# GateLoop attention and a squared-ReLU block on one core: a complex product summed on VectorE instead of TensorE, and a planner that charges TensorE for its stops

## The chip, the cores and the metric

The kernel runs on one core of a Trainium2 chip. The core has TensorE (PE in the profile), VectorE (DVE), ScalarE (ACT), GpSimd (POOL) and SyncE (SP), each with a queue of its own that is worked off in order, and 16 DMA engines that all queues share. The metric is the device time of one execution in microseconds, lower is better; the time before is 726.08 us, the median of three runs (725.42, 726.08 and 728.75).

## What is computed

A complex recurrence runs over 768 time steps, for 4 batches of 8 heads of 48 channels. Its result, reshaped to 3072 tokens of 384 values, goes through two matrix products with a squared ReLU between them. The weights come as float64 and everything else as float32.

```python
scale = np.minimum(mag, 0.999) / (mag + 1e-06)        # mag = |a|
a_re_n, a_im_n = (a_re * scale, a_im * scale)
for t in range(S):
    ar, ai = (a_re_n[:, :, t, :, None], a_im_n[:, :, t, :, None])
    new_re = ar * S_re - ai * S_im
    new_im = ar * S_im + ai * S_re
    kv = np.einsum('bhd,bhe->bhde', k[:, :, t], v[:, :, t])
    S_re, S_im = (new_re + kv, new_im)
    y[:, :, t] = np.einsum('bhd,bhde->bhe', q[:, :, t], S_re)
...
h = x @ w_in                     # x: (3072, 384), w_in: (384, 2048)
r = np.maximum(h, 0.0)
g = r * r
return (g @ w_out).astype(np.float32)
```

## The kernel before

The 3072 tokens are cut into six units of 512 tokens (`NU = 6`). A unit has 128 blocks of four time steps; a block is a partition, and its four steps times 384 channels lie along the free axis, in two halves of heads (z = 0 and 1). Each unit goes through three stages.

**The chain** (`chain`, line 882) makes the running product of the complex decays. `roots`, `normalise` and `inner` work within the blocks, on VectorE and ScalarE, and leave each block's total in the tile `xn`, real part in row 0 and imaginary part in row 1. What is then wanted is the running product of these totals over the 128 blocks, a product along partitions. So `totals` turns `xn` on TensorE (three transposes for each of the two rows, line 1008, with a permutation in place of the identity, so that the blocks come out sorted for a scan); ScalarE copies the turned totals to `e`; `scan` multiplies them up on VectorE in levels, in many small instructions (lines 1121 to 1177); and its last level multiplies `e` (four groups of partial products) by `incx` (the prefix of each group). This last product is complex: each of its two rows is a sum of two real products. `last` (line 1184) forms them with four multiplications of 128x384 and writes the two terms of each row apart, into `gg`, which lies in `KC[0]`. It puts them down in the order of the blocks, and for that the elements that one instruction writes one after the other lie 16 elements apart. `back` then turns each row back to one block per partition, and adds the two terms at the same time: `turned` (line 1000) issues, for each of three pieces of 128 columns, two ordinary matmuls with the identity that accumulate in PSUM (line 1011). ScalarE copies the result to `xn` (line 1205). `apply` (lines 1243, 1247, 1250, 1257) multiplies it into decays, queries and keys, and `gather` (line 1297) regroups the keys by DMA into `KC`.

**The pairs** (`pairs`, four pairs of heads) compute the linear attention: transposes of q and k (`turn_pe`, line 1356, with a ScalarE copy at 1360, for units 0 and 1; DMAs for the others), scores (1374) masked on VectorE (1377), states (`keep`, 1402, 1411, 1413), and the outputs (`mix`, 1426 and 1430), which ScalarE copies to `yt` (1436) and DMAs carry to `xT` (1444).

**The dense part** (`dense`) takes the unit in two groups of 256 tokens: 16 x 3 matmuls of 128x256 with the first weights (1466), squared ReLU on ScalarE (1497, 1498), and the second product, in 32 matmuls of 128x384 per group for unit 0 (1512), and in matmuls of 128x192 with sums on VectorE (`half` at 1563, `put` at 1578, `add` at 1587) for the others. In unit 0 the weights are converted from float64 as they arrive (`convert`: ScalarE at 788 and 792, VectorE at 794, 798, 801).

No scheduler orders any of this. Every piece of work is a **step** with a cost in microseconds, written by hand (`plan.add`), the keys that it reads and writes, and a rank. `Plan.order` runs through the steps as a list scheduler does: an engine takes, of the steps whose inputs are done, the one with the lowest rank (PAIR 1, CHAIN 2, DENSE 3; the dense part's relu, copies and sums 0), and the order in which it takes them becomes the order of the engines' queues. So a cost in the plan doesn't change how long anything takes; it changes which instruction stands before which. A step of TensorE with an input from another engine counts as ready only `MARGIN` 0.6 us after that input (`SLACK` 2 us after some DMAs), beside a `HOP` for each engine. The dense matmuls of unit n have the lowest rank on TensorE, and so fill the places where the chain and the pairs of unit n+1 leave TensorE free.

```python
step("PE", 0.12 * NM * len(terms), keys, [(b,)], go, rk)                    # turned
step("DVE", 2 * tt(384) + 0.55, E + I, [("KC", 0, "r", r)] + ([] if r else K), last, ahead)
```

Of the kernel before, what the change touches and what calls it, by code (L numbers as in the profile page):

```python
# [15 lines left out]
ALU = mybir.AluOpType  # L16
# [464 lines left out]
class Plan:  # L481
# [3 lines left out]
    MARGIN = 0.6  # L485
    SLACK = 2.0
    RATE = 280e3

    def __init__(self):
        self.steps = []  # L490
# [25 lines left out]
    def order(self):  # L516
        steps = self.steps
        users = [[] for _ in steps]
        left = []
        for n, s in enumerate(steps):  # L520
            left.append(len(s[2]))
            for d in s[2]:
                users[d].append(n)
        engines = {s[0] for s in steps}
        free = {e: 0.0 for e in engines}
        wait = {e: [] for e in engines}
        done, start, at = {}, {}, {}
        bus = 0.0

        def ready(n):  # L530
            e = steps[n][0]
            t = 0.0
            for d in steps[n][2]:
                same = steps[d][0] == e and steps[d][5] is None
                hop = 0.0 if same else self.HOP[steps[d][0]]
                if e == "PE" and not same and done[d] > 100.0:
                    paired = steps[d][5] is not None and steps[n][6]
                    hop += self.SLACK if paired else self.MARGIN
                t = max(t, done[d] + hop)
            at[n] = t  # L540
            wait[e].append(n)

        for n in range(len(steps)):
            if not left[n]:
                ready(n)
        for _ in steps:
            best = None
            for e in engines:
                if not wait[e]:
                    continue  # L550
                t = max(free[e], min(at[n] for n in wait[e]))
                if best is None or t < best[0]:
                    best = (t, e)
            t, e = best
            n = min((n for n in wait[e] if at[n] <= t), key=lambda n: (steps[n][4], n))
            wait[e].remove(n)
            _, dur, _, _, _, wire, _ = steps[n]
            start[n] = t
            free[e] = t + dur
            if wire is None:  # L560
                done[n] = t + dur
            else:
                lat, size = wire
                bus = max(bus, t + dur) + size / self.RATE
                done[n] = max(bus, t + dur) + lat
            for m in users[n]:
                left[m] -= 1
                if not left[m]:
                    ready(m)
        self.start, self.done = start, done  # L570
        return sorted(start, key=lambda n: (start[n], n))
# [10 lines left out]
def fast_path(ctx, tc, q, k, v, a_re, a_im, moe_w_in, moe_w_out, out, flag):  # L582
# [6 lines left out]
    C = 128  # L589
# [5 lines left out]
    DM = H * D  # L595
    FF = moe_w_in.shape[1]
    NM = DM // C
# [13 lines left out]
    dve, pool, act, sp = nc.vector, nc.gpsimd, nc.scalar, nc.sync  # L611
    pe = nc.tensor
# [5 lines left out]
    def sb(name, n, dtype=F32, rows=C):  # L618
# [9 lines left out]
    DH = DM // 2  # L628
# [3 lines left out]
    KC = [sb(f"KC{z}", W * HH * R) for z in range(2)]  # L632
    vv = [sb("v0", W * H * D), TT[:, 2 * NT * DH:]]
    e = sb("e", 3 * DM).rearrange("p (r w g) -> p r w g", r=3, w=4)
    el = sb("el", 3 * NM).rearrange("p (r m) -> p r m", r=3)
    x = sb("x", NM * (C + 1)).rearrange("p (m c) -> p m c", m=NM)
# [4 lines left out]
    xn = sb("xn", 3 * DM).rearrange("p (r n) -> p r n", r=3)  # L641
# [12 lines left out]
    ident = sb("ident", C)  # L654
    perm = sb("perm", C)
# [12 lines left out]
    bank = {n: psum.tile([C, 512], F32, name=n)  # L668
            for n in ("d0", "d1", "d2", "sc0", "sc1", "tr0", "tr1", "yp")}
# [30 lines left out]
    def tt(n):  # L700
        return n / 960.0 + 0.07
# [9 lines left out]
    def step(*args, **kw):  # L711
        return plan.add(*args, **kw)
# [159 lines left out]
    def chain(n):  # L872
# [9 lines left out]
        ahead = (CHAIN, n - 0.01)  # L882
# [114 lines left out]
        fresh = ps_[0][3] == 0  # L997
        ends = ps_[-1][3] + ps_[-1][1] * W == S

        def turned(terms, put, by, keys, rk):  # L1000
            b = trs[slot["tr"] % 2]
            slot["tr"] += 1

            def go():
                for m in range(NM):
                    dst = put(bank[b][:, 0:DM], m)
                    if len(terms) == 1:
                        pe.transpose(dst, terms[0](m), by)
                    else:
                        for i, src in enumerate(terms):  # L1010
                            pe.matmul(dst, lhsT=src(m), rhs=by, start=(i == 0),  # L1011
                                      stop=(i == len(terms) - 1))
            step("PE", 0.12 * NM * len(terms), keys, [(b,)], go, rk)
            return bank[b][:, 0:DM], (b,)

        def natural(t, m):
# [3 lines left out]
            return t.rearrange("p (y m k) -> p m y k", m=NM, k=8)[:, m]  # L1020

        def totals(j):
            ps, b = turned([lambda m: xn[:, j, ts(m, C)]], spread, perm,
                           [("xn", j, 0), ("xn", j, 1)], ahead)
            p4 = ps.rearrange("p (w g) -> p w g", w=4)
            last = ps.rearrange("p (y m k) -> p y m k", m=NM, k=8)[:, 0, :, 0]
            step("ACT", ac(DM), [b], [("e", j)], lambda: act.copy(
                out=e[:, j], in_=p4), ahead)
            if j == 1:
                step("ACT", ac(DM), [b], [("e", 2)], lambda: act.mul(  # L1030
                    out=e[:, 2], in_=p4, mul=-1.0), ahead)
            if not ends:
                step("ACT", ac(NM), [b], [("el", j)], lambda: act.copy(
                    out=el[:, j], in_=last), ahead)
                if j == 1:
                    step("ACT", ac(NM), [b], [("el", 2)], lambda: act.mul(
                        out=el[:, 2], in_=last, mul=-1.0), ahead)

            def start():
                first = SCALE if j == 0 else 0.0  # L1040
                head = e[:, j, 0].rearrange("p (x m k) -> p x m k", x=4, m=NM)[:, 0]
                if fresh:
                    dve.memset(head[:, :, 0], first)
                else:
                    dve.tensor_copy(out=head[:, :, 0], in_=ce[:, j])
                if cross:
                    dve.memset(head[:, :, 4], first)
            step("DVE", 0.12, [("ce",)], [("e", j)], start, ahead)
# [90 lines left out]
        def scan():  # L1139
# [37 lines left out]
                dve.tensor_copy(out=x4[:, 0:2, 0], in_=tx[:, 0:2])  # L1177
                minus(incx)
            step("DVE", 0.36, I, I, finish_inc, ahead)

            for r in range(2):
                def last(r=r):
                    for f, y, ro in ((gg[0], 0, r), (gg[1], 2 - r, 1 - r)):
                        dve.tensor_tensor(
                            out=f[:, r].rearrange("p (g x w) -> p w x g", x=4, w=4),
                            in0=e[:, ro].rearrange("p w (x g) -> p w x g", x=4),
                            in1=incx[:, y].rearrange("p (x g) -> p x g", x=4).unsqueeze(
                                1).to_broadcast([C, 4, 4, 24]), op=ALU.mult)
                step("DVE", 2 * tt(384) + 0.55, E + I, [("KC", 0, "r", r)] + ([] if r else K),
                     last, ahead)  # L1190
            if not ends:
                tail = [f.rearrange("p r (m k y) -> p r m k y", m=NM, k=8)[:, :, :, 7, 15]
                        for f in gg]
                tl = few[:, 0:6].rearrange("p (r m) -> p r m", r=2)
                step("DVE", 0.15, K + [("KC", 0, "r", 0), ("KC", 0, "r", 1)], [("tl",)],
                     lambda: dve.tensor_tensor(out=tl, in0=tail[0], in1=tail[1], op=ALU.add),
                     ahead)
                product(ce, tl, lambda lo, hi: el[:, lo:hi],
                        [("tl",), ("el", 0), ("el", 1), ("el", 2)], [("ce",)],
                        few[:, 6:18], [("tl",)], late[1])  # L1200

        def back(j):
            terms = [lambda m, f=f: f[:, j, ts(m, C)] for f in gg]
            ps, b = turned(terms, natural, ident, K + [("KC", 0, "r", j)], ahead)
            step("ACT", ac(DM), [b], [("xn", j, 0), ("xn", j, 1)], lambda: act.copy(  # L1205
                out=xn[:, j], in_=ps), ahead)

# [368 lines left out]
    def put(n, o, x0, x1, op, h):  # L1576
        sl = slice(4 * h, 4 * h + 4)
        step("DVE", tt(4 * C), gk(x0, h) + gk(x1, h), gk(o, h), lambda: dve.tensor_tensor(  # L1578
            out=g4[:, o, sl], in0=g4[:, x0, sl], in1=g4[:, x1, sl], op=op), (0, n))
# [4 lines left out]

    def add(n, o, c, c0, b, o0=None):
        o0 = o if o0 is None else o0
        step("DVE", tt(DH) + 0.1, [("ot", o0, c0), (b,)], [("ot", o, c)], lambda: dve.tensor_tensor(  # L1587
            out=ots[o][:, ts(c, DH)], in0=ots[o0][:, ts(c0, DH)], in1=bank[b][:, 0:DH],
            op=ALU.add), (0, n))

# [158 lines left out]
```

## Time and profile before

| | |
|---|---|
| median of three runs | 726.08 us |
| the profiled execution: its own time | 726.25 us |
| the profiled execution: span, first to last instruction | 724.4 us |
| PE busy, of the span | 654.7 us (90%), 4226 records |
| DVE busy | 573.3 us (79%), 1176 records |
| ACT busy | 360.2 us (50%), 579 records |
| POOL busy | 176.3 us (24%), 333 records |
| PE L1011, the matmuls that turn and add | 144 records |
| DVE L1184, the multiplications of the last product | 24 records, 17.2 us, mean 814 ns |
| granted TensorE clock, mean | 0.982 |

The records of an engine are its instructions as the profiler saw them; one float32 matmul leaves two records, a transpose one. A group's line gives the count, the busy time, the mean duration of one record and the idle time of the engine just ahead of it. Successive records of one engine overlap: a PE record of 128x128 lasts 272 ns, while the next one begins after about 0.11 us. The distance from start to start is then what an instruction takes from its engine, and a merged row of the timeline with so many records gives it when the next row's start is subtracted. The chain of waits lists such distances directly. Line numbers here and below are those of the kernel before.

### The profile page before, as it was taken

The numbers are of one execution on the slowest core, as the hardware profiler recorded it, in microseconds if no ns is written. First come the engines' busy times: TensorE is split into PE (matmuls) and PEld (weight loads), VectorE is DVE, ScalarE is ACT, GpSimd is POOL, SyncE is SP. The second block draws the span as 40 slices with busy tenths as digits, with TensorE's granted clock in tenths as the row PEclk, the third lists the DMA queues.
The fourth block names the chain that finished last, engine by engine and source line by source line (L and its number), as shares of the span: only waits on it lengthen the run. The fifth ranks groups of instructions, "written<-read, shape, count | busy, mean of one in ns | idle before, by whom it ended". The sixth has DMA issues, their size and how long they took to land.

```text
span 724.4 us, 11842 instructions
## 1 busy us (share of the span) xinstructions
PE 654.7 (90%) x4226; PEld 589.5 (81%) x4226; DVE 573.3 (79%) x1176; ACT 360.2 (50%) x579; POOL 176.3 (24%) x333
## 2 busy tenths in 40 slices
PE   0037789899999999999999999999999999999996
PEld 0036678668778998999999998998999989999995
DVE  5987999899879589788899588998797997356621
ACT  6783457965575704448613658423578142122230
POOL 6504154052400003314036050033050033041100
PEclk9995899999999999999999999999999999999999
DMA  9731359320531004744018661027460045287400
GB/s 287 243 122 46 75 132 251 110 66 18 156 106 28 1 12 107 185 115 132 1 36 216 148 130 41 1 66 190 129 164 1 1 118 130 59 319 252 171 1 27
DMA packets 56358, 79.55 MB, mean 110 GB/s; under 512 B 10945, under 2 KB 38465, under 8 KB 56289
## 3 DMA queue, kind: packets, MB, share of 16 engines
q0 software_dynamic: 15232, 40.72, 18.6%
q1 hardware_dynamic: 36928, 32.98, 18.0%
q10 hardware_dynamic: 4128, 4.98, 2.7%
q8 instruction: 36, 0.59, 0.4%
q14 instruction: 34, 0.27, 0.1%
HBM read 48.76 MB, written 4.72 MB: 74 GB/s over the span
## 4 chain that ended last, share of the span: by engine, by line
PE 83%; DVE 6%; ACT 4%; SPq 1%; DMA 1%; issue 1%; DVEq 0%; ACTq 0%
PE d L1466 30%; PE d L1563 26%; PE sc L1374 5%; PE d L1512 5%; PE tr L1402 3%; PE yp L1426 3%; PE tr L1011 2%; PE yp L1430 2%; SPq L1297 1%; PE sc L1466 1%; DMA xT<-yt 1%; PE tr L1356 1%; PE d L1356 1%; DVE f L947 1%; PE tr L1466 1%
## 5 line engine op out<-in xcount | busy, mean ns | idle before, releaser
L1466 PE MATMUL d<-xT,w 128*128 128x256 f32 x1056 | 238.1, 382 | 4.5 <-DMA xT<-yt 3.4
L1466 PEld LDWEIGHTS d<-xT,w 128*128 128x128 f32 x1056 | 199.2, 191 | 32.2 <-issue 4.5
L1563 PE MATMUL d<-w,g 128*128 128x192 f32 x768 | 132.4, 327 | 0.0
L1563 PEld LDWEIGHTS d<-w,g 128*128 128x128 f32 x768 | 125.1, 190 | 0.9 <-issue 0.6
L1497 ACT ACTIVATE g<-d 128x512 f32<-128x512 f32 x88 | 52.5, 597 | 127.0 <-PE d L1466 113.8
L1297 POOL DMA_DIRECT2D KC<-f x160 | 78.7, 499 | 120.4 <-DVE f L1257 46.5
L1578 DVE TENSOR_TENSOR g<-g 128x512 f32<-128x512 f32 x64 | 43.4, 688 | 35.2 <-ACT g L1498 23.5
L868 POOL DMA_DIRECT2D v<-in_v_dram x80 | 47.0, 594 | 86.7 <-PE yp L1430 47.2
L1563 PE MATMUL d<-T,g 128*128 128x192 f32 x384 | 67.1, 326 | 0.0
L1524 POOL DMA_DIRECT2D out_dram<-ot x22 | 12.6, 573 | 207.5 <-DVE ot L1587 111.8
L1563 PEld LDWEIGHTS d<-T,g 128*128 128x128 f32 x384 | 62.9, 190 | 0.2 <-issue 0.2
L1498 ACT ACTIVATE g<-g 128x512 f32<-128x512 f32 x96 | 60.7, 633 | 3.1
L1374 PE MATMUL sc<-QT 96*128 96x128 f32 x368 | 47.9, 285 | 1.3 <-ACT QT L1360 1.3
L1374 PEld LDWEIGHTS sc<-QT 96*128 96x128 f32 x368 | 45.1, 198 | 4.4 <-ACT QT L1360 2.2
L1243 DVE TENSOR_TENSOR f<-aq,xn 128x384 f32<-128x384 f32 (+1 forms) x64 | 45.2, 751 | 1.9 <-ACT xn L1205 1.9
L1436 ACT COPY yt<-yp 112x512 f32<-112x512 f32 x24 | 26.3, 1095 | 40.0 <-PE yp L1430 40.0
L1257 DVE TENSOR_TENSOR f<-aq 128x384 f32<-128x384 f32 (+1 forms) x64 | 45.4, 753 | 0.7
L1512 PE MATMUL d<-w,g 128*128 128x384 f32 x128 | 43.9, 489 | 1.6 <-DVE w L801 1.6
L1587 DVE TENSOR_TENSOR ot<-ot,d 128x192 f32<-128x192 f32 x64 | 21.8, 350 | 25.9 <-PE d L1563 25.0
L1377 DVE TENSOR_TENSOR A<-sc,mask 128x512 f32<-128x512 f32 x45 | 30.0, 682 | 10.8 <-PE sc L1374 10.6
L947 DVE TENSOR_TENSOR f<-aq 128x384 f32<-128x384 f32 x72 | 37.0, 555 | 1.0
L1512 PEld LDWEIGHTS d<-w,g 128*128 128x128 f32 x128 | 23.3, 190 | 15.3 <-DVE w L801 2.0
(193 smaller groups left out, 1012.5 us busy)
## 6 DMA issues: line engine op xcount, KB each, us to landing
QT<-aq SPq DMA_DIRECT2D x128, 64.0 KB, 2.1
f<-in_moe_w_in_dram POOLq DMA_DIRECT2D x8, 768.0 KB, 7.4
f<-in_moe_w_out_dram POOLq DMA_DIRECT2D x8, 768.0 KB, 5.1
KC<-f POOLq DMA_DIRECT2D x104, 48.0 KB, 2.3
out_dram<-ot POOLq DMA_DIRECT2D x22, 192.0 KB, 2.6
QT<-aq ACTq DMA_DIRECT2D x64, 64.0 KB, 2.3
v<-in_v_dram POOLq DMA_DIRECT2D x80, 48.0 KB, 3.5
xT<-yt SPq DMA_DIRECT2D x36, 96.0 KB, 2.4
```

What stands on the lines that cost most here:

```text
L868: lambda i=i, c=c, src=src: pool.dma_start(out=t[32 * c:32 * c + 32, i], in_=src[c]), vrank, 32 * 1536, 4.0,
L947: dve.tensor_tensor(out=f, in0=a[:, :, :, c - 1], in1=a[:, j, :, c].unsqueeze(1).to_broadcast([C, 2, HH, D]), op=ALU.mult)
L1243: lambda j=j, r=r: dve.tensor_tensor(out=f4[:, j, r], in0=a[:, r], in1=over(j), op=ALU.mult), late[z])
L1257: lambda j=j, r=r, o=o: dve.tensor_tensor(out=o[:, :, :, r * D:(r + 1) * D], in0=qk[:, j], in1=a[:, r], op=ALU.mult), late[z])
L1297: lambda i=i, c=c, queue=queue: queue.dma_start(out=kc[32 * c:32 * c + 32, i], in_=nat[32 * i:32 * i + 32, c]),
L1374: pe.matmul(sa[:, j], lhsT=T[:, j, 1, h], rhs=T[:, j, 0, h], start=True, stop=True)
L1466: pe.matmul(ps, lhsT=w1[:, f // FP, m, ts(f % FP, C)], rhs=xT[:, n % 2, m, ts(grp, G)], start=(m == 0), stop=(m == NM - 1))
L1497: act.activation(out=o, in_=ps, func=AF.Relu)
L1498: act.activation(out=o, in_=o, func=AF.Square)
L1512: pe.matmul(ps, lhsT=gt[:, f % 2, ts(i, C)], rhs=w2[:, f], start=(f == 0), stop=(f == NF - 1))
L1563: pe.matmul(bank[b][:, 0:DH], lhsT=g4[:, r, j], rhs=w(j), start=first and j == 0, stop=last and j == NT - 1)
L1578: step("DVE", tt(4 * C), gk(x0, h) + gk(x1, h), gk(o, h), lambda: dve.tensor_tensor(out=g4[:, o, sl], in0=g4[:, x0, sl], in1=g4[:, x1, sl] ...
```

## The change

It has three parts.

1. **The last product.** `last` now writes its two terms in the scan's own order, one element after the other, and a third VectorE instruction adds them, writing the sum to `xn` in the order of the blocks. The step's cost in the plan goes from `2 * tt(384) + 0.55` to `3 * tt(384) + 0.28`, and both rows now name the whole of `K` among the keys that they write. `back` turns `xn` instead of two terms: `turned` has one source, so it issues three transposes for a row instead of six accumulating matmuls, and its cost in the plan goes from 0.72 to 0.36. The carry for the next unit (`tl`) becomes a copy from `xn` instead of an addition (line 1196).
2. **The planner.** When a TensorE step would start more than 2.5 us after the end of the one before, it and those that follow within 3.4 us are charged up to double their cost, in the plan alone.
3. **A cost.** The sums of the dense part (`add`, line 1587) are planned at 0.01 us above `tt(192)` instead of 0.1.

```diff
@@ class Plan
+    STOP, COLD = 2.5, 3.4
@@ Plan.order
-        bus = 0.0
+        bus = warm = 0.0
...
             start[n] = t
+            if e == "PE":
+
+                if t > free[e] + self.STOP:
+                    warm = t + self.COLD
+                if t < warm:
+                    dur += min(dur, 0.5 * (warm - t))
             free[e] = t + dur
@@ chain
-        def turned(terms, put, by, keys, rk):
+        def turned(src, put, by, keys, rk):
...
                 for m in range(NM):
-                    dst = put(bank[b][:, 0:DM], m)
-                    if len(terms) == 1:
-                        pe.transpose(dst, terms[0](m), by)
-                    else:
-                        for i, src in enumerate(terms):
-                            pe.matmul(dst, lhsT=src(m), rhs=by, start=(i == 0),
-                                      stop=(i == len(terms) - 1))
-            step("PE", 0.12 * NM * len(terms), keys, [(b,)], go, rk)
+                    pe.transpose(put(bank[b][:, 0:DM], m), src(m), by)
+            step("PE", 0.12 * NM, keys, [(b,)], go, rk)
@@ scan
             for r in range(2):
                 def last(r=r):
-                    for f, y, ro in ((gg[0], 0, r), (gg[1], 2 - r, 1 - r)):
+                    own = [f[:, r].rearrange("p (w x g) -> p w x g", w=4, x=4) for f in gg]
+                    for o, y, ro in ((own[0], 0, r), (own[1], 2 - r, 1 - r)):
                         dve.tensor_tensor(
-                            out=f[:, r].rearrange("p (g x w) -> p w x g", x=4, w=4),
-                            in0=e[:, ro].rearrange("p w (x g) -> p w x g", x=4),
+                            out=o, in0=e[:, ro].rearrange("p w (x g) -> p w x g", x=4),
                             in1=incx[:, y].rearrange("p (x g) -> p x g", x=4).unsqueeze(
                                 1).to_broadcast([C, 4, 4, 24]), op=ALU.mult)
-                step("DVE", 2 * tt(384) + 0.55, E + I, [("KC", 0, "r", r)] + ([] if r else K),
-                     last, ahead)
+
+                    dve.tensor_tensor(
+                        out=xn[:, r].rearrange("p (g x w) -> p w x g", x=4, w=4),
+                        in0=own[0], in1=own[1], op=ALU.add)
+                step("DVE", 3 * tt(384) + 0.28, E + I, K + [("xn", r, 0), ("xn", r, 1)], last,
+                     ahead)
             if not ends:
-                tail = [f.rearrange("p r (m k y) -> p r m k y", m=NM, k=8)[:, :, :, 7, 15]
-                        for f in gg]
+                tail = xn[:, 0:2].rearrange("p r (m k y) -> p r m k y", m=NM, k=8)[:, :, :, 7, 15]
...
-                     lambda: dve.tensor_tensor(out=tl, in0=tail[0], in1=tail[1], op=ALU.add),
+                     lambda: dve.tensor_copy(out=tl, in_=tail), ahead)
@@ back
-            terms = [lambda m, f=f: f[:, j, ts(m, C)] for f in gg]
-            ps, b = turned(terms, natural, ident, K + [("KC", 0, "r", j)], ahead)
+            ps, b = turned(lambda m: xn[:, j, ts(m, C)], natural, ident,
+                           [("xn", j, 0), ("xn", j, 1)], ahead)
@@ add
-        step("DVE", tt(DH) + 0.1, [("ot", o0, c0), (b,)], [("ot", o, c)], lambda: dve.tensor_tensor(
+        step("DVE", tt(DH) + 0.01, [("ot", o0, c0), (b,)], [("ot", o, c)], lambda: dve.tensor_tensor(
```

The call of `turned` in `totals` loses the list around its source as well, and is otherwise as it was.

## The prediction

> **What bounds the kernel now.** I read the page first: the busy tenths of the 40 slices.
>
> ```profile
> span 724.4 us, 11842 instructions
> ...
> PE   0037789899999999999999999999999999999996
> ...
> DVE  5987999899879589788899588998797997356621
> ...
> PEclk9995899999999999999999999999999999999999
> ```
>
> VectorE leads through the first six slices (some 107 us) while TensorE waits; from then on TensorE stands at 9 to the end. The table of busy times by stretch says how full those nines are (length, then PE, PEld, DVE, ACT, POOL):
>
> ```profile
> 46.00:107.00 61.00, 46.06 (x348) 40.35 (x349) 53.74 (x119) 31.35 (x46) 20.36 (x40) 0.83 0.29 69
> 107.00:145.00 38.00, 35.30 (x147) 28.11 (x146) 35.18 (x57) 32.35 (x44) 9.43 (x14) 0.96 0.65 182
> ...
> 178.00:231.00 53.00, 52.38 (x381) 40.69 (x379) 43.82 (x80) 33.27 (x53) 11.38 (x23) 1.00 0.37 104
> ...
> 436.00:537.00 101.00, 101.00 (x682) 94.22 (x681) 86.85 (x181) 49.63 (x83) 20.69 (x40) 1.00 0.37 98
> ```
>
> After 107 us TensorE is idle for 2.7 us before 145 and 0.6 us before 231, and not at all from there to the last matmuls. VectorE has 9.2 and 14.2 us to spare in the last two of these stretches, and 2.8 in the second. So a microsecond taken off TensorE after 107 us comes off the end, as long as nothing makes it wait. TensorE's timeline shows the stops, and the work in dispute:
>
> ```profile
> 135.15 2.86 PE L1466 MATMUL d<-xT,w 128*128 128x256 f32 x12 [1.12 <-ACT g L1497]
> 139.58 4.14 PE L1512 MATMUL d<-w,g 128*128 128x384 f32 x12 [1.57 <-DVE w L801]
> 143.56 0.82 PE L1008 MATMUL tr<-perm,xn 128*128 128x128 f32 x6
> 144.21 14.36 PE L1512 MATMUL d<-w,g 128*128 128x384 f32 x44
> ...
> 161.00 2.84 PE L1011 MATMUL tr<-ident,KC 128*128 128x128 f32 x24
> 163.67 1.68 PE L1466 MATMUL d<-xT,w 128*128 128x256 f32 x7
> ```
>
> From start to start, 24 records of line 1011 take 2.67 us (0.111 each; 12 to a row), and 6 transposes of line 1008 take 0.65 us (0.108). In the later units the chain of waits has the same price for one row's turn:
>
> ```profile
> 262.52 1.34 PE tr L1011 x12
> 263.86 1.30 PE d L1563 x8
> 265.16 1.34 PE tr L1011 x12
> ```
>
> **What the Trainium skill says.** "TensorE: Matmul & The Clock Gate", Part 4: PE-mode transpose, gives a transpose some 275 ns in a kernel; the trace has 272 to 273 ns for line 1008, of which it holds TensorE for 0.108. Part 1 of the same page halves the clock after an idle window of about 3.4 us and for about as long afterwards. The trace agrees in kind: after a stop of 2.64 us the dense part's first 10 records take 4.08 us, where 10 take 2.16 us later. "VectorE: DVE Perf Modes", The TRN2 errata, prices a float32 tensor_tensor at (N+151)/0.96 ns, 557 for N = 384; line 947 has 555. "SBUF — State Buffer", Door 1, says that an access pays for each new 16-byte line; line 1184, which writes 64 bytes apart, has 814 ns at the same size:
>
> ```profile
> L947 DVE TENSOR_TENSOR f<-aq 128x384 f32<-128x384 f32 x72 | 37.0, 555 | 1.0
> ...
> L1184 DVE TENSOR_TENSOR KC<-e,yt 128x384 f32<-128x384 f32 x24 | 17.2, 814 | 0.0
> ```
>
> **TensorE's part.** A row's turn falls from 12 records to 3: 1.34 - 3 x 0.109 = 1.01 us. Units 1 to 5 have ten rows: -10.1 us, -2.0 in unit 1 and -8.1 in units 2 to 5. The plan had charged 0.72 for what took 1.34; it now charges 0.36 for 0.33, so TensorE runs less behind its plan. The wait margins (0.6 us) stay.
>
> **VectorE's part.** Four multiplications take 2.78 us before, 0.66 from start to start, so 1.32 a row. After: two in order at 0.47 (the start-to-start distance of the other 128x384 rows), about 0.11 for the add's wait on the second (at 149 us, line 1125 starts 0.38 after 1123, and 1123 starts 0.28 after 1121), and the add, which writes 64 bytes apart: 0.66. Together 1.71, +0.39 a row. If the add wrote for 0.47, +0.20; if it paid twice the surcharge, +0.58. That is +4.7 us over twelve rows, beside an engine that is not the bound in units 2 to 5: cost nothing. The cover is TensorE's dense work left between the last pair of a unit and the next xT: after the mixes ending at 321, 421, 525 and 630 us, 9 to 14 us of line 1563 follow. The chain in fact shortens, by 2 x 1.01 - 2 x 0.39. Were the cover gone, it would cost 0.8 us per unit. In unit 0 the adds lie on the path, but the half-clocked turn there (24 records in 5.6 us, 46.55 to 52.2) ends sooner, and VectorE's 0.89 us wait for its ScalarE copy goes. About nothing. The copy of the carry replaces an add of six elements (0.17 us): nothing. The cheaper plan cost of line 1587 (0.28; start to start it is 0.27) takes away slack that the plan had by mistake; nothing by itself.
>
> **The order.** The changed kernel, built and not run, shows where instructions moved. I take them by stage.
>
> Before 107 us: VectorE's stops of 1.55, 0.55, 0.80 and 0.59 us (65 to 72 us, each for TensorE) get the later 975 and 977 put into them. Adding up the new queue with the durations above, the second half's first keys (1257) are out at about 86.0 instead of 86.85. SyncE then issues 16 gathers of 0.64 us (87 to 98 us) and four loads before the xT transfers, all in the old order, so the dense part starts 0.85 us sooner. Against it, ScalarE squares the next unit's decays (902) ahead of the last yt copy, and has to wait for a load that lands near 104; the last xT piece may come 2 us later. It had about 2.7 us in hand (landed 108.7, wanted 111.4), and the new queue puts one more pair of matmuls ahead of it. I take -0.85; bounds -3 and +1.5.
>
> 107 to 145 us: the third piece of the second weights is fetched and converted ahead of the fourth and fifth, where before it came after both (the fourth done at 133.4, the fifth at 135.7, the third at 139.5), and the dense block behind the late relu moves back. That fits the order in which 1512 wants the pieces, so I let both stops (1.12 and 1.57) go: -2.7; bounds -2.7 and 0, nothing below, since there is no more to gain.
>
> Unit 1's pairs (178 to 231 us): here the gain meets a limit. The fillers among these pairs are what is left of 1512. Before, 32 of its 64 instructions came ahead of the first turn of the pairs; in the new order 40 do. Eight instructions, 16 records of 0.323 us, 5.2 us, are then missing among the pairs, and pairs 2 and 3 have nearly none. Each pair turns q and k through two banks with a ScalarE copy of 0.58 us between, which nothing covers now: I count waits of about 0.4 ahead of pair 2's scores, 0.8 between two turns in one bank, 0.45 ahead of pair 3's last turn, 0.9 ahead of its scores, and 0.3 for xT. Sum +2.9; bounds 0 and 5.5, which eats all that TensorE had gained by then (0.85 + 2.7 + 2.0). The wait for xT at 231.09 (0.7) stays, and is late next.
>
> Units 2 to 5: the order changes in places of a few matmuls; nothing either way.
>
> **Sum.** -0.85 - 2.7 - 2.0 + 2.9 - 8.1 = -10.75 us. The profiled execution took 726.25 us (span 724.4 and 1.85 around it), 0.17 above the median: 715.5 us.
>
> **Rivals.**
> - *Unit 1's pairs are covered.* The copies end in time, as they did before (0.9 to 2.8 us from a copy's end to its reader). Then all -13.65 remain: 712.6. For it: TensorE's margins in the plan. Against it: the missing 5.2 us.
> - *Unit 1 is latency-bound.* Neither the start nor the conversions pay, since dense work of unit 1 restarts at 231 whatever TensorE saved. Only units 2 to 5 gain: 718.1. For it: the wait for xT stands there already.
> - *The order loses.* As the second, and the late xT piece (2 us) and new stops in units 2 to 5 eat most of the 8.1: about 724.
> - *The clock drops: slower.* Waits in unit 1's pairs, with transposes between, count as idle, and TensorE falls to half clock from pair 1 on. A pair's own TensorE work is about 6.1 us (16 turns, 16 score, 12 state and some 28 output records), so three pairs cost 18.3, and the dense restart 2: -13.65 + 2.9 + 20.3 = +9.5, 735.8. It decides from about 12.5 us of work at half clock, two pairs. For it: 60 to 68 us, where unit 0's transposes and scores ran at half rate (32 records in about 8 us). Against it: single waits below 1 us.
> - *It isn't done.* The built queue has three transposes a row and three VectorE instructions, so this falls away.
>
> **How the numbers follow.** Forecast 0.56 (713.5 to 717), pairs covered 0.20, latency-bound 0.16, order loses 0.05, clock 0.03. The range 710.5 to 720.5 takes in the bounds of the start and of unit 1's waits, and leaves out the last two cases and some tails. This kernel's measurement tells about 0.5% (3.6 us) from no change: faster 0.92, same 0.05, slower 0.03.
>
> **What would show it.** Line 1011 with 36 records at about 0.11 from start to start; line 1184's row at about 1.71 us; no stop near 135 and 139; the first dense matmul behind its xT wait near 105.8; several stops of 0.3 to 1 us on TensorE between pair 2 and the xT wait of unit 1, that wait ending near 228.4; none from there on. A stop of over 1 us in units 2 to 5, or records of double length after 178 us, would make it wrong.

## The result, and the profile after

The changed kernel took 722.02 us (median, 719.49 to 725.35) against 725.87 us for the kernel before, run beside it: ratio 0.995, interval 0.993 to 0.9969. It is faster by 3.9 us, half a per cent; I had predicted 10.6. The profiled execution took 724.28 us (span 722.6), 2.0 under that of before, so the traces show about half of what the medians do.

The page of the changed kernel, the span and the busy tenths of the 40 slices:

```profile
span 722.6 us, 11635 instructions
...
PE   0017798999998999999999999999999999999996
...
PEclk9999899999998999999999999999999999999999
```

TensorE's row and its clock have an 8 in the slice from 217 to 235 us, where both had a 9 before. The table of busy times by stretch (us, then PE, PEld, DVE, ACT and POOL busy, PEclk, DMA share, GB/s) says how much that is:

```profile
178.00:231.00 53.00, 48.14 (x342) 37.63 (x343) 39.40 (x75) 30.10 (x48) 12.65 (x26) 0.94 0.36 102
...
221.00:232.00 11.00, 10.28 (x62) 9.10 (x63) 7.37 (x11) 6.01 (x11) 0.00 (x0) 0.69 0.04 10
436.00:537.00 101.00, 101.00 (x677) 94.14 (x676) 90.20 (x186) 52.05 (x88) 19.90 (x39) 1.00 0.37 97
```

In unit 1's pairs (178 to 231 us) TensorE now stands still for 4.9 us, where it did for 0.6, and between 221 and 232 us the granted clock is 0.69. In units 2 to 5 it is as full as it was. The timeline of TensorE (start, duration, engine, line, operation, count, and in brackets the idle time before it and what ended it) shows the same stretch record by record. The changed kernel's lines are shifted: 1358 is the turn of before's 1356, 1376 the scores of 1374, 1468 the dense part of 1466, 1514 that of 1512, 1362 the copy of 1360, 808 the last step of a conversion (801).

```profile
213.36 0.64 PE L1358 MATMUL tr<-ident,f 128*96 128x128 f32 x4 [0.67 <-ACT QT L1362]
...
215.14 0.31 PE L1428 MATMUL yp<-A,T 128*48 128x128 f32 x1 [0.79 <-DVE A L1379]
...
219.63 0.64 PE L1358 MATMUL tr<-ident,f 128*96 128x128 f32 x4 [1.54 <-ACT QT L1362]
221.72 3.75 PE L1376 MATMUL sc<-QT 96*128 96x128 f32 x16 [1.44 <-ACT QT L1362]
...
225.82 4.20 PE L1468 MATMUL d<-xT,w 128*128 128x256 f32 x12
```

Three of these four stops end with a copy by ScalarE. Behind them, 16 score records take 3.75 us and 12 dense records 4.20, where the same kinds take 2.05 (at 209.90 us) and 2.75 (at 125.74 us). This is TensorE at half clock, at which each record takes about twice as long. ScalarE's own timeline says why its copies are late:

```profile
215.81 0.51 ACT L969 COPY xn<-aq 128x384 f32<-128x384 f32 x1 [2.51 <-DVE aq L962]
216.23 0.57 ACT L1362 COPY QT<-tr 96x512 f32<-96x512 f32 x1
216.71 1.48 ACT L974 ACTIVATE f<-aq 128x1536 f32<-128x1536 f32 x1
218.10 1.06 ACT L1438 COPY yt<-yp 112x512 f32<-112x512 f32 x1
218.95 0.63 ACT L1362 COPY QT<-tr 96x512 f32<-96x512 f32 x1
219.48 0.84 ACT L978 ACTIVATE f<-f 128x768 f32<-128x768 f32 x1
220.35 0.84 ACT L980 ACTIVATE f<-f 128x768 f32<-128x768 f32 x1
221.10 0.56 ACT L1362 COPY QT<-tr 96x512 f32<-96x512 f32 x1
```

Between two copies of the pair (1362) stand steps of unit 2's chain (969, 974, 978, 980), and one of them waits 2.51 us for VectorE with a copy queued behind it. TensorE's last two stops end 0.05 us behind the ends of the copies that start at 218.95 and 221.10 us: the first of these stood behind 974 and a copy of `yt` (1438), the second behind 978 and 980. In the kernel before, the same neighbours were there; but TensorE had dense records of unit 0 to do until the copy came. Here the last of these, line 1514, starts at 208.3 us (before, line 1512: 219.8).

The new instructions themselves are as foreseen. A row's turn in TensorE's timeline, and ahead of it the longest of the stops that unit 0's dense part has now:

```profile
109.89 1.13 PE L1468 MATMUL sc<-xT,w 128*128 128x256 f32 x4 [2.27 <-DVE w L808]
...
160.94 0.49 PE L1013 MATMUL tr<-ident,xn 128*128 128x128 f32 x3
161.27 1.46 PE L1468 MATMUL d<-xT,w 128*128 128x256 f32 x6
```

The turn holds TensorE for 0.33 us (160.94 to 161.27). VectorE's multiplications, from the groups (count, busy us, mean ns), and the add, from its line (least, median, most ns):

```profile
L1185 DVE TENSOR_TENSOR KC<-e,yt 128x384 f32<-128x384 f32 x24 | 12.2, 550 | 0.0
```

```profile
L1190 DVE TENSOR_TENSOR xn<-KC x12: 811/816/832, 45.9 to 567.2; 128x384 f32<-128x384 f32 x12
```

### The profile page after: what moved, and what is told of

It reads as the page before. It is cut to its first block, busy times and chain, and to the rows that moved or that the text cites. A ratio compares the mean times of both kernels' runs of the same rounds, so it can differ in the third digit from the quotient of the medians.

```text
span 722.6 us, 11635 instructions
## 1 busy us (share of the span) xinstructions
PE 647.1 (90%) x4118; PEld 579.3 (80%) x4118; DVE 576.7 (80%) x1188; ACT 359.1 (50%) x579; POOL 176.1 (24%) x333
## 4 chain that ended last, share of the span: by engine, by line
PE 76%; DVE 14%; ACT 3%; DMA 2%; SPq 2%; issue 1%; POOL 0%; DVEq 0%
PE d L1468 29%; PE d L1565 26%; PE sc L1376 5%; PE d L1514 4%; PE tr L1404 3%; PE yp L1428 3%; DVE f L954 3%; PE yp L1432 2%; DVE aq L935 1%; PE tr L1013 1%; PE d L1358 1%; DMA KC<-f 1%; DVE f L1259 1%; DVE aq L960 1%; DVE f L1245 1%
## 5 line engine op out<-in xcount | busy, mean ns | idle before, releaser
L1565 PE MATMUL d<-w,g 128*128 128x192 f32 x768 | 132.2, 327 | 0.0
L1376 PE MATMUL sc<-QT 96*128 96x128 f32 x368 | 49.9, 292 | 2.1 <-ACT QT L1362 2.1
L1438 ACT COPY yt<-yp 112x512 f32<-112x512 f32 x24 | 26.3, 1097 | 25.2 <-PE yp L1432 25.2
L1013 PE MATMUL tr<-perm,xn 128*128 128x128 f32 x36 | 6.1, 303 | 32.7 <-ACT xn L969 31.6
```

Of the source, the lines that this page charges most:

```text
L1376: pe.matmul(sa[:, j], lhsT=T[:, j, 1, h], rhs=T[:, j, 0, h], start=True, stop=True)
L1565: pe.matmul(bank[b][:, 0:DH], lhsT=g4[:, r, j], rhs=w(j), start=first and j == 0, stop=last and j == NT - 1)
```

## The experiments

Medians are each against the kernel before, run beside it. The last two columns come from the one profiled execution of each: first the time from unit 0's first dense record to the restart of unit 1's dense part (the record that its wait for xT holds back; "the restart" in what follows), then from there to the end of the matrix products, less before's 486.2. I count from unit 0's dense part because what lies ahead of it varies by 4 us from one execution to another (last section). "Ahead" is the number of the 64 last dense instructions of unit 0 (line 1512, in what follows: the fillers) that stand ahead of unit 1's first pair in the built queue.

| run | median us | less before's | ratio and interval | ahead | to unit 1's dense part | rest |
|---|---|---|---|---|---|---|
| before | 725.9 | | | 32 | 127.8 | 0 |
| changed | 722.0 | -3.9 | 0.995 (0.993-0.997) | 40 | 132.2 | -6.5 |
| e1 new instructions, old order | 719.3 | -6.2 | 0.991 (0.988-0.994) | 32 | 127.3 | -6.0 |
| e9 old instructions, new order | 730.4 | +4.9 | 1.006 (1.004-1.009) | 40 | 132.7 | +1.3 |
| e2 product with its own costs | 723.8 | -1.7 | 0.997 (0.995-0.999) | 40 | 133.4 | -8.2 |
| e3 double steps alone | 731.6 | +6.1 | 1.007 (1.005-1.010) | 42 | 132.2 | +2.8 |
| e4 changed, no double steps | 724.0 | -1.6 | 0.998 (0.996-1.000) | 40 | 131.9 | -7.7 |
| e5 changed, fillers held | 717.5 | -7.9 | 0.988 (0.985-0.992) | 32 | 129.0 | -8.3 |
| e6 e5, no double steps | 722.1 | -3.3 | 0.993 (0.990-0.996) | 32 | 129.4 | -8.0 |
| e7 changed, kept warm | 719.8 | -5.6 | 0.992 (0.989-0.995) | 40 | 129.4 | -6.8 |
| e8 before, less dense work | 724.2 | -1.2 | 0.998 (0.996-1.000) | 24 of 56 | 126.7 | +0.2 |
| e10 held, 36 ahead | 716.3 | -9.3 | 0.987 (0.984-0.990) | 36 | 127.6 | -8.3 |
| e11 held, 40 ahead, spread | 717.9 | -7.7 | 0.990 (0.986-0.993) | 40 | 124.7 | -5.3 |
| e12 e5, short conversions | 716.7 | -8.8 | 0.987 (0.984-0.991) | 32 | 128.4 | -8.3 |
| e13 e12, none on ScalarE | 717.5 | -7.3 | 0.990 (0.986-0.993) | 32 | 127.8 | -8.3 |

My theory after the result: the order took the gain, because the fillers were spent ahead of unit 1's pairs. The rivals: unit 1 is bound by its chain whatever the order; the new instructions cost something that I had not counted; or ScalarE's queue, fillers or not.

**Instructions and order apart (e1, e9).** e1 has the changed kernel's product and turn, with the planned costs and keys of before and without the doubled steps (the main lines of the edit):

```diff
-                step("DVE", 3 * tt(384) + 0.28, E + I, K + [("xn", r, 0), ("xn", r, 1)], last,
-                     ahead)
...
+                step("DVE", 2 * tt(384) + 0.55, E + I, [("KC", 0, "r", r)] + ([] if r else K),
+                     last, ahead)
...
-            step("PE", 0.12 * NM, keys, [(b,)], go, rk)
+            step("PE", dur, keys, [(b,)], go, rk)
```

`dur` is 0.24 * NM for the turns of `back`.

> The new instructions (ordered products, one add, three transposes a row, the carry copied row by row) with the planned costs of before, so that every engine's queue stands in the order of before, apart from those instructions. Theory A (the order took the gain: the fillers among unit 1's pairs were spent ahead of them): the ten rows of units 1 to 5 pay their 1.0 us each, ratio 0.986 (about -10 us), no half clock after 178 us, and 24 of the 64 last instructions of unit 0's dense work still to come at the first pair of unit 1 plus 8 as before. Theory B (unit 1 is bound by its chain whatever the order, so only units 2 to 5 pay): 0.989, about -8. Theory C (the new instructions cost something themselves that I did not count, in the chain of unit 1 or at the start): 0.994 to 0.996, about the whole change's own -3 to -4.

Measured -6.2 us, between B and C, and nearest to B: unit 1's dense part restarts 0.5 us sooner, although TensorE saved 2.0 us on its turns. Units 2 to 5 give 6.0 instead of 8.1, since in this order units 4 and 5 now wait for transfers (0.65 us at 514 us, DMA QT<-aq, and 0.33 us at 617 us).

e9 is the reverse: the changed order with the four strided multiplications and turns of 12 records put back into the steps:

```diff
-                    pe.transpose(put(bank[b][:, 0:DM], m), src(m), by)
...
+                        for i, t in enumerate(terms):
+                            pe.matmul(dst, lhsT=t, rhs=by, start=(i == 0),
+                                      stop=(i == len(terms) - 1))
```

> The changed kernel's order in every queue, with the instructions of before in it: four multiplications that write in the order of blocks, the carry as an add, and turns of 12 records. With the first run this closes a square: new instructions in the old order gave 0.991 (-6 us), both together 0.995 (-4). If the two add up, the order alone costs +2 to +3 us, 1.003 to 1.005. If the order only costs because TensorE is faster in it: 1.000.

The order alone costs 4.9 us, more than the 2 to 3 of the forecast: the parts don't simply add up (-6.2 and +4.9 against -3.9 together). In the trace 4.9 us of it lie in unit 1 (132.7 against 127.8) and 1.3 behind. It has the same stops there as the changed kernel, 1.55 and 1.44 us for ScalarE's copies. So the loss in unit 1 needs no new instruction.

**Which part orders so (e2, e3, e4).** e3 is the kernel before with the lines of STOP and COLD, e4 the changed kernel without them, e2 the changed kernel without them and with the old cost of the dense sum. The edit of e2:

```diff
-            if e == "PE":
-                if t > free[e] + self.STOP:
-                    warm = t + self.COLD
-                if t < warm:
-                    dur += min(dur, 0.5 * (warm - t))
...
-        step("DVE", tt(DH) + 0.01, [("ot", o0, c0), (b,)], [("ot", o, c)], lambda: dve.tensor_tensor(
+        step("DVE", tt(DH) + 0.1, [("ot", o0, c0), (b,)], [("ot", o, c)], lambda: dve.tensor_tensor(
```

> The product's part of the change with its new planned costs and keys, but without the doubled steps behind stops and with the old cost of the dense sum. 40 of the 64 last dense instructions of unit 0 stand ahead of unit 1's first pair, where the order of before has 32. Theory A (too few fillers left among unit 1's pairs): about the whole change's result, -2 to -5 us (0.993 to 0.997), with stops and half clock in unit 1's pairs. Theory that the doubled steps behind stops (left out here) cause the loss: about -10 (0.986).

> The kernel of before with the doubled planned steps behind stops alone; no instruction differs, only the order. 42 of 64 dense instructions stand ahead of unit 1's first pair. Theory A: no TensorE time is saved, so the pairs starve and the run is slower, +3 to +7 us (1.004 to 1.010). If the gain at 107 to 145 us is real and unit 1 does not starve: -2 to -3 us (0.997).

> The changed kernel without the doubled steps behind stops (product and dense sum's cost stay). 40 fillers stand ahead of unit 1's first pair, as in the changed kernel. Theory A: within 2 us of the changed kernel, 0.993 to 0.997 of before. If the doubled steps are what costs: 0.986 to 0.989.

Theory A's side came in all three: +6.1 as forecast, -1.7 (e2) and -1.6 (e4) at or just past the edge of the numbers. Either part alone takes 40 or 42 fillers ahead of the first pair, and unit 1's dense part is then 4 to 6 us late. In e3, where TensorE is not relieved anywhere, that is 4.4 us, and 2.8 more come behind it.

**The fillers held back (e5, e6, e10, e11).** To the changed kernel's plan a constraint is added: the fillers from number m on may not be taken before turn k of unit 1.

```diff
+    for k, m in enumerate([16, 16, 18, 18, 19, 20, 20, 22, 23, 24, 24, 26, 27, 28, 28, 31]):
+        plan.hold(fill[m:], turns[k])    # adds turns[k] to what fill[m:] depend on; two instructions each
```

> The changed kernel with one thing added to the plan: the last 32 of unit 0's 64 last dense instructions may not be taken before the turns among which the kernel before had them (32 stand ahead of unit 1's first pair again, instead of 40). Instructions and units 2 to 5 stay as in the changed kernel. Theory A (the change loses its gain because the fillers among unit 1's pairs are spent ahead of them): the dense part of unit 1 restarts within 1 us of where it did before, instead of 3.6 us later, and the run is 3 to 4 us under the changed kernel: 0.989 to 0.991 of before. Rival (ScalarE's queue, where the copies of the pairs stand behind the next unit's chain, makes the loss, fillers or not): as the changed kernel, 0.994 to 0.996.

-7.9 us: theory A, and its interval lies below the changed kernel's. The restart is 1.2 us later than before's, where the forecast allowed 1. TensorE has no stop over 0.4 us among the pairs. It has one ahead of them:

```profile
170.50 0.42 PE L1364 MATMUL tr<-ident,f 128*96 128x128 f32 x2 [0.72 <-DVE f L1265]
173.91 1.51 PE L1364 MATMUL tr<-ident,f 128*96 128x128 f32 x6 [2.98 <-DVE f L1265]
```

The 3.7 us by which TensorE is early are spent waiting for VectorE's products, the last link of unit 1's chain. That is the time into which the changed kernel had put its fillers.

> As the run before it, without the doubled steps behind stops. Theory A: the same within 1.5 us. If the doubled steps are what orders the first 145 us better: 1 to 2 us slower than with them.

Neither came: the medians are 4.6 us apart, though the intervals overlap. From unit 0's dense part on the traces differ by only 0.7 us; the rest lies ahead of it. There the clock differs: from 78 to 98 us it is 0.66 in the traces of e2, e4 and e6, which have the product's new instructions and costs without the doubled steps, and 0.83 to 0.91 in the changed kernel, e5, e7 and e10 to e13, which have the doubled steps too. (In e1, with the costs of before, it is 0.91.) In the medians e4 is 1.9 us slower than the changed kernel. So with the new costs the doubled steps seem to pay there, by some 2 to 5 us; with one trace of each kernel and overlapping intervals this is not shown.

e10 and e11 change only the list of numbers (18, 18, 19, 20, ... and 20, 20, 21, 21, ...).

> As the run with the fillers held, but 36 of 64 stand ahead of unit 1's first pair instead of 32, the rest among the pairs. With 32 TensorE stood still for 3.7 us ahead of the first pair (waiting for VectorE's products) and had no stop among the pairs. If unit 1's pairs are TensorE's own work then, the four instructions (2.6 us) fill that stop: -2 to -2.6 against the run with 32, 0.985 of before. If fewer fillers bring the stops among the pairs back: no gain, 0.988 or above.

> 40 of 64 stand ahead of unit 1's first pair, as in the changed kernel, but the last 24 are spread over all four pairs instead of being used up by the last pair's turns (62 ahead of the last turn instead of 64 from the second pair's end on). If it is where the fillers lie among the pairs that counts: near the run with 32, 0.987 to 0.989. If it is how many are left: 0.992 to 0.994.

e10 has the lowest median of all, 716.3 us, ratio 0.987: it beats both kernels. Against e5 it gains 1.4 us in the traces where 2 to 2.6 were forecast, and the intervals overlap. What is left of the stop, and the dense records behind it:

```profile
177.36 0.86 PE L1364 MATMUL tr<-ident,f 128*96 128x128 f32 x6 [2.03 <-DVE f L1265]
178.06 2.58 PE L1522 MATMUL d<-w,g 128*128 128x384 f32 x4
```

Four such records take 1.46 us otherwise: this stop too is followed by half clock.

e11 decides a point: with 40 ahead, as many as in the changed kernel, but 24 spread over all pairs, it gives -7.7. Not how many stand ahead, but that the last pairs still have some, is what counts. Its dense part of unit 1 restarts soonest (124.7), and part of that is lost again: at 240.56 us TensorE stops 2.25 us for ScalarE's g.

**The clock (e7).** Junk products in the stops of the last pair:

```diff
+    def junk_matmuls(k):
+        for f in range(k):
+            pe.matmul(bank["d0"][:, 0:DM], lhsT=w2[:, f, 0:C], rhs=w2[:, f], start=True, stop=True)
```

> The changed kernel with five junk matrix products (128x384, 0.65 us each at full clock) put into the stops of unit 1's last pair: one ahead of the second turn, two ahead of the fourth, two ahead of the first scores. What they write is overwritten. The waits stay as they are. If the half clock after those stops is the larger part of the loss in unit 1 (I count 3.5 us for it in the changed kernel's trace): 2 to 3.5 us under the changed kernel, 0.990 to 0.992 of before. If the waits for ScalarE's copies are what costs and the half clock only fills them: the changed kernel's time within 1 us, 0.994 to 0.997.

In TensorE's timeline of this run the junk is line 1315 (its first pair of records went ahead of the third turn that ran):

```profile
215.45 1.52 PE L1315 MATMUL d<-w 128*128 128x384 f32 x4
...
217.24 1.46 PE L1315 MATMUL d<-w 128*128 128x384 f32 x4
218.55 2.05 PE L1385 MATMUL sc<-QT 96*128 96x128 f32 x16
...
220.74 2.82 PE L1477 MATMUL d<-xT,w 128*128 128x256 f32 x12
```

From the last pair's first turn to its scores it takes 9.66 us (208.89 to 218.55), as in the changed kernel (9.64): the waits are untouched, only filled. But the scores take 2.05 instead of 3.75 us and the dense records 2.82 instead of 4.20: 3.1 us of half clock gone. The restart of unit 1's dense part is 2.8 us sooner, and the gain 1.7 us larger than the changed kernel's (5.6 against 3.9). The intervals of the medians overlap; it is the trace that shows the half clock's part.

**What binds unit 1 (e8, e12, e13).** e8 is the kernel before with less TensorE work ahead of the pairs:

```diff
-                    for f in (2 * part, 2 * part + 1):
+                    for f in (2 * part, 2 * part + 1)[:1 if grp == 0 and i == 1 else 2]:
```

> The kernel before with eight of unit 0's dense instructions left out (16 records of 0.323 us, 5.2 us of TensorE's work between 140 and 160 us; every second block of one output tile's sum, so that tile is not the reference's); the order is otherwise untouched. If unit 1 is bound by its chain and pairs (nothing that TensorE saves ahead of unit 1's pairs pays): 0 to -1.5 us, 0.998 to 1.000. If TensorE's queue is the bound there, as my prediction took it: -5 us, 0.993.

-1.2 us in the median, 1.1 in unit 1: of the 5.2 us left out, four fifths come back. The first of the new waits is 1.60 us for VectorE's product at 153.8 us, and 22 records of the turn behind it take 4.35 us, at half clock, where 24 took 2.84 before. So TensorE's queue is not the bound there: TensorE arrives early and waits for the chain. But some 1.7 us of what comes back (an estimate from these durations) is the half clock behind that wait and not the wait, and e8 does not say what the saving would be worth with the clock kept up.

e12 and e13 take work from the other two engines, in e5's order. The edit of e12; e13 treats ScalarE's two steps of these conversions in the same way:

```diff
-        step("DVE", tt(PW), keys + [("lo", i, int(mixed))], wk, lambda: dve.tensor_tensor(
-            out=bits, in0=bits, in1=lo, op=ALU.add), rank)
+        step("DVE", tt(PW), keys + [("lo", i, int(mixed))], wk, lambda: i >= NPIECE or
+             dve.tensor_tensor(out=bits, in0=bits, in1=lo, op=ALU.add), rank)
```

> The run with the fillers held at 32, with VectorE's last step of the eight conversions of the second weights left out (the low words are not added, so the weights are those of the high words alone): 8 x 0.96 us of VectorE's work less between 115 and 143 us, order as it was. If VectorE sets the time of unit 1's pairs (first its conversions, then its chain): TensorE's stops of 3.7 us ahead of unit 1's first pair shrink or go, -3 to -4 against the run with 32, 0.983 to 0.984. If something else does (the transfers, ScalarE): as that run, 0.988.

> The run with the short conversions, with ScalarE's steps of the same eight conversions left out as well (8 x 0.9 and 6 x 1.92 us between 95 and 138 us; the low words are not used at all, the weights are as in that run); order as it was. In that run VectorE stood still for 9.2 us waiting for ScalarE's conversions, and the first pair of unit 1 came no earlier. If ScalarE's queue is what sets unit 1's chain: the chain starts some 9 us sooner, TensorE's stop of 3.0 us ahead of the first pair goes, and the run is 2.5 to 4 us under that one, 0.982 to 0.984 of before. If the stretch of the chain itself (from its first copy to the first pair) is the bound and its start is set by the transfers: as that run, 0.987.

Neither did what was hoped. The first pair comes 1.1 us sooner in both traces (its first turns end their wait 72.7 us behind unit 0's first dense record, 73.8 in e5), not 3 to 9; the stop for VectorE's products is 2.98 us in both, and the medians are e5's within the intervals. In e12 VectorE then waits 9.2 us for ScalarE's conversions; in e13, with those gone, ScalarE's timeline shows the next link:

```profile
135.91 2.85 ACT L981 ACTIVATE f<-aq 128x1536 f32<-128x1536 f32 x2
145.87 0.48 ACT L1035 COPY e<-tr 128x384 f32<-128x384 f32 x1 [7.10 <-PE tr L1020]
```

Line 1020 is the first turn of unit 1's chain. It stands in TensorE's queue behind unit 0's dense work. In e5, with the conversions in place, the same copy waits 0.65 us for its turn. So TensorE's queue up to 145 us, the conversions on VectorE and those on ScalarE end close together, and behind the last of them comes a chain of some 30 us to the first pair. I expected one engine to be the bound; for the start of the chain there is none. For the chain itself the traces point to VectorE. Here is its row of the table by stretch in the kernel before (columns as above):

```profile
145.00:178.00 33.00, 33.00 (x152) 25.51 (x151) 31.07 (x88) 20.28 (x41) 11.94 (x22) 1.00 0.17 39
```

VectorE is busy for 31.1 of 33 us, and for 28.3 of 30 in e5 (145 to 175 us, where TensorE has 26.3). It waits for another engine for 0.4 us of the first stretch and not at all in the second. What e12 takes from VectorE lies ahead of this stretch, so no run shortens it. That less VectorE work between the chain's first turn and the first pair would pay is argued from these rows and not shown; nor did I try to move that turn ahead.

## Why the prediction was wrong, step by step

**TensorE's part** held. 36 records of line 1013 with ident, 0.33 us a row; from each unit to the next the dense part gains 2.02 us on that of before (units 3 to 5). Over units 2 to 5 that is -8.1. The trace shows -6.5 behind unit 1's restart, since a stop of 1.05 us for ScalarE's g came in at 250.6 us, and about 0.5 that I did not trace. In e5, e10, e12 and e13 it is -8.3.

**VectorE's part** held: 1.79 us a row (157.74 to 159.53) against 1.71; the add takes 816 ns, the multiplications in order 550. It is hidden in units 2 to 5, as said. In unit 1 I had no term for it, and there it stands in the queue that the first pair waits for: two rows add 2 x 0.47 us to a VectorE that is busy for 28.3 of 30 us (e5).

**The order, before 107 and 107 to 145.** The two stops of 1.12 and 1.57 us went, as forecast, and one of 0.69 took their place. The dense part started without its 2.64 us stop for xT, more than the 0.85 I took, and gave it back at once: 2.27 and 0.80 us for conversions (line 808), stops that I did not have. The first of line 1514 stands at 128.33 us, 0.36 sooner. At unit 1's first turn the sum was nevertheless good: I had -0.85 - 2.7 - 2.0 + 5.2 = -0.35 us, it was +0.49 (178.46 against 177.97), with the eight more fillers done. That it came so near is in part luck: the start gave more than I had, and the conversions took it back.

**Unit 1's pairs** is the step that failed. I had +2.9, bounds 0 and 5.5. From the first turn to the dense restart TensorE runs the same records in both kernels, apart from the 16 of the fillers: 53.1 us before, 57.5 after, and there are 5.2 us less of fillers in it, so 9.5 us were lost. The stops are 5.4 us where before had 0.7 (+4.7). I had counted five waits at 0.3 to 0.9. Four came where I had them, at 0.67, 1.54, 1.44 and 0.59; instead of the one ahead of pair 2's scores there is one of 0.38 ahead of pair 1's, and one of 0.79 for VectorE's `A` I had not foreseen. Each costs 0.15 to 0.2 us more from start to start than the timeline shows as idle, about 1 in all. Half clock is 3.1, which e7 took away. Some 0.7 us is left without a cause.

Two errors of reasoning stand behind it. I priced the copies at their own 0.58 us, and not with what is queued ahead of them on ScalarE, which waits for VectorE. And I kept the drop of the clock for a rival that needed two whole pairs at half rate; it came for 32 records (16 of scores, 4 of states, 12 dense ones). The case against it, "single waits below 1 us", was wrong by half a microsecond.

**What I counted as won ahead of the pairs** was not. The forecast takes -5.55 us up to there, and gives 2.9 of it back. It rests on the sentence that a microsecond taken off TensorE after 107 us comes off the end, and the table under that sentence left out the stretch after 107 us (145 to 178, shown above) in which VectorE has least to spare, 1.9 us. e8 shows that 5.2 us less of TensorE's work is worth 1.1. e1, e5 and e10, without stops among the pairs, restart unit 1's dense part at -0.5, +1.2 and -0.2. Counted in the same way, from unit 0's first dense record, the forecast's own terms without the waits give -2.0 for e1 and -4.7 for e5 and e10. This is the second rival, *unit 1 is latency-bound* (718.1): its time is right for the orders that keep their fillers (716.3 to 719.3 in e1, e5, e10 and e11), though e11 shows that the restart itself can come 3.1 us sooner. The changed kernel has its mechanism, and the starved pairs on top. The plan fills every gap of TensorE at once with what is ready; what was saved ahead of a stage that waits for a chain thus took fillers out of that stage.

"A stop of over 1 us in units 2 to 5, or records of double length after 178 us, would make it wrong": both happened, at 250.6 us (behind the restart, where the forecast's units 2 to 5 begin) and at 221.7 us.

## What to carry to other kernels

Time saved on an engine ahead of a stage that starts with a chain of other engines may not be won: here the greedy order turned it into filler work done early, and the stage was then bare. A table of busy times that is to show the bound must have every stretch in it. After a change of a planner's costs, count how much independent work is still left in each such stage, its last part above all, and hold it back there if need be: here that made 0.995 into 0.987 to 0.990. A copy that no other work covers costs what is queued ahead of it on its engine, waits included, and here a run of such waits cost TensorE's clock too (3.1 us).

## What the runs showed of the hardware

The Trainium skill ("TensorE: Matmul & The Clock Gate", Part 1) speaks of an idle window of about 3.4 us. Here shorter stops were followed by half clock. In the changed kernel the clock fell to half at 221.72 us with no stop over 1.54 us: 4.4 us of idle time in four stops, within 9.6 us. 2.98 us of e5 at 174 us had the same effect (6 turns in 1.51 us). So had 2.03 us of e10 at 177 us, a little later: its 6 turns take 0.86 us, the four dense records behind them 2.58, and the granted clock is 0.51 from 178.2 to 181.7 us. (The prediction's first case compares 4.08 us, to the end of the last record, with 2.16 from start to start; from start to start it is 3.92.)

Which way it falls can differ with the same queue. The changed kernel, e5, e7 and e10 to e13 have one TensorE queue as far as 16 dense records near 110 us, a little behind a stop for the converted weights. The 16 take 3.62, 3.62 and 3.69 us in the changed kernel, e5 and e11, behind stops of 2.27, 1.95 and 1.65 us; in e7, e10, e12 and e13 they take 5.16, 5.31, 5.14 and 5.30 us, behind stops of 2.11, 2.22, 2.27 and 1.99. The same 2.27 us thus went both ways.

There is an earlier case. Ahead of unit 0's first scores TensorE waits 3.09 us and then 0.7 in both of these executions: the kernel before, and e8, which has the same queue up to 120 us.

```profile
64.45 3.78 PE L1374 MATMUL sc<-QT 96*128 96x128 f32 x16 [0.67 <-ACT QT L1360]
```

```profile
63.95 2.05 PE L1374 MATMUL sc<-QT 96*128 96x128 f32 x16 [0.71 <-ACT QT L1360]
```

The second is at full rate in the scores, and its unit 0's dense part starts at 99.3 us instead of 103.3. That is about half the spread of one kernel's times (721.9 to 730.6 us for before), and it is why single traces were compared from that point on.
